# Attention followed by a Silu layer pair: a new order of loads, shifts and exponentials for the first batch

## The chip, the cores and the metric

The kernel runs on one core of a Trainium2 chip. The metric is the device time of one execution in microseconds; it was 334.84 (median of three runs, 333.54 to 335.08) before the change. A core has TensorE (PE, matrix products; its weight loads are shown as PEld), VectorE (DVE), ScalarE (ACT), GpSimd (POOL) and SyncE (SP). Transfers between memory and the core's SBUF run on 16 DMA engines; POOL and SP issue them here.

## The reference

Eight batches of eight heads, 576 positions, 64 features a head. Heads 0 to 3 see the 32 positions up to their own ("plain"), heads 4 to 7 every fourth position of the last 128 ("dilated"). The output of the attention, all heads of a position side by side (512 wide), goes through a layer of 2048 with h * sigmoid(h), and back to 512.

```python
scores = scale * np.matmul(q, k.transpose(0, 1, 3, 2))
mask_plain = (rel >= 0) & (rel < window)                       # window = 32
mask_dil = (rel >= 0) & (rel < window * dilation) & (rel % dilation == 0)   # dilation = 4
scores = np.where(masks[None, :, :, :], scores, -1000000000.0)
scores = scores - np.max(scores, axis=-1, keepdims=True)
attn = np.exp(scores)
attn = attn / (np.sum(attn, axis=-1, keepdims=True) + 1e-09)
x = np.matmul(attn, v)            # then (batch, position, head * feature)
h = x @ w_in
g = h * (1.0 / (1.0 + np.exp(-h)))
out = (g @ w_out).astype(np.float32)
```

## The kernel before

All products are in 16 bits with 32-bit sums. For each batch the kernel does attention in two kinds, z = 0 (plain heads) and z = 1 (dilated heads, as four classes of positions). Queries come in blocks of 32, each against a stretch of 64 keys. The steps of one kind are functions: `transpose` or `transpose0` (q and k turned by PE, copied out of PSUM by `copy`), `scores` or `scores0` (products, then on DVE the mask and the negated row maximum), `shift` (DVE adds the maximum, so that one exponential does for all blocks), `exps` (ACT: one exponential if `shift` was called, otherwise one for each of 8 to 12 blocks, each with a read of its row sum), `normal` (DVE: row sums if shifted, reciprocal, product), `turn` and `turned` (PE turns the weights, a copy brings them back), `values` or `values0` (products with v), `finish` or `finish0` (copies into xT). Then come layer 1 (`layer1`, `layer1_part`: products with w_in, Silu on ACT into gT) and layer 2 (`layer2_first`, `layer2`: products with w_out, a DVE copy, a store by SP).

Batch 0 is special. It runs in two parts of positions: part 0 is positions 0 to 255, part 1 the rest. `load_qk0`, `transpose0`, `scores0`, `values0`, `finish0` and `layer1_part` take the part. Its first half is written out by hand at the end of the kernel. The second half is placed by `plan_of(0)` between the pieces of layer 1: `at(s, fn, ...)` puts a call at step s, and `plan(s)` calls what stands there. Layer 1 of part 0 has steps -16 to -1 (a pair of f tiles each two steps), part 1 has 0 to 15, layer 2 has 16 to 31; the calls for batch 1 stand there too. In this way the program order of each engine is fixed. An engine takes its instructions in this order, and one that waits holds back those behind it.

The values are held in `vw`, one tile for each of two batches. Its rows 64 to 127 (KB to P) hold v as loaded, with 36 column blocks for the plain heads (h * 9 + m) and 16 for each of three dilated groups. Rows 32 to 63 and 0 to 31 hold the same shifted by 32 and 64 rows. `shift_v` makes them, in the parts `FIRST` (column blocks m 0 to 3 of the plain heads, first dilated group: what part 0 needs), `REST`, or `ALL`. For batch 0 the kernel before does this with seven DMAs on SP.

All loads of q, k, v, w_in and w_out are issued by POOL, since they change the type from 32 to 16 bits. Their order is: `load_qk0(0)`, the identity and band masks (POOL's own work), `load_qk0(1)`, v of batch 0, first dilated group and plain heads (L123, L136), w_in chunk 0 (L173), v's second and short groups (L123, L131), w_in chunks 1, 2, 3, the eight transfers of `load_qk(1)` (L102), `clear_v(1)` (memsets, L187 to L190), w_out chunks 0 and 1 (L179), `load_v(1)`, w_out chunks 2 and 3, and `load_qk(2)` (L102).

PSUM is held as two tiles `big` of two banks (fillers, batch 0's scores, h, o) and four tiles `ps` of one. `keep_busy` (L795) runs products of the identity with itself, whose results nobody reads: 96 of 32 columns at the start, 12 and 6 of 128 columns before and after the first values. `layer2_first` (L632 on) holds four output tiles t as halves of two `big` tiles, `o2[t // 2][:, t % 2]`, goes through four rounds c of four f tiles each, and stores t in the last round with `store` (L650).

Of the kernel before, what the change touches and what calls it, by code (L numbers as in the profile page):

```python
# [27 lines left out]
def kernel(  # L28
# [112 lines left out]
    def shift_v(b, queue, parts):  # L141

        vw = vws[b % 2]
        f = vw[:, 0:NP].rearrange("p (h m) d -> p h m d", h=HH)
        for m0, m1, n in parts:
            queue.dma_start(
                out=vw[W:KB, NP + n.start * ND : NP + n.stop * ND],
                in_=vw[KB : KB + W, NP + n.start * ND : NP + n.stop * ND],
            )
            if n.stop == 2:  # L150
                queue.dma_start(
                    out=vw[0:W, NP + ND : NP + 2 * ND], in_=vw[KB + W : P, NP : NP + ND]
                )
            queue.dma_start(out=f[W:KB, :, m0:m1], in_=f[KB : KB + W, :, m0:m1])
            l0 = max(m0, 1)
            queue.dma_start(out=f[0:W, :, l0:m1], in_=f[KB + W : P, :, l0 - 1 : m1 - 1])

    FIRST, REST, ALL = (0, 4, slice(0, 1)), (4, NM, slice(1, 2)), (0, NM, slice(0, 2))

# [9 lines left out]
    qk0 = {}  # L169
    FC = DFF // 4  # L170

    def load_w_in(c):
        nc.gpsimd.dma_start(  # L173
            out=w_in16[:, :, c * FC : (c + 1) * FC],
            in_=moe_w_in[:, c * FC : (c + 1) * FC].rearrange("(c p) f -> p c f", p=P),
        )

    def load_w_out(c):
# [88 lines left out]
    def to_classes(a, which, i, t0, t, copy):  # L267

        e, n = t.shape[1], t.shape[3]
        dst, i0 = ((a["qC"], 0), (a["kC"], W))[which]  # L270
        i0 += t0 // DIL
        copy(
            dst[:, 2 * i : 2 * i + 2, :, i0 : i0 + n * e].rearrange("d h r (p e) -> d (h r) p e", e=e),
            t.rearrange("d e m p -> d m p e"),
        )

    def transpose0(part, hp, which, copy):

# [4 lines left out]
        if hp >= HP // 2:  # L283
            t = t.rearrange("d (e m) p -> d e m p", m=4)
            for h in (0, 1):
                for u in range(0, UR, 2):
                    nc.tensor.transpose(
                        t[:, u // DIL, 2 * h + u % DIL // 2, :],
                        src[0:n, 2 * hp + h, u : u + 2, :].rearrange("p u d -> p (u d)"),
                        ident[0:n, 0:n],  # L290
                    )
            return to_classes(a, which, hp - HP // 2, t0, t, copy)
        for u in range(UR):
            for hi in (0, 1):
                nc.tensor.transpose(  # L295
                    t[hi * D : hi * D + D, u, :], src[0:n, 2 * hp + hi, u, :], ident[0:n, 0:n]
                )
        o = (a["qT"][:, hp], a["kT"][:, hp, W:])[which][:, t0 : t0 + n * UR]
        copy(o.rearrange("d (p u) -> d p u", u=UR), t.rearrange("d u p -> d p u"))

    def score(b, hp, hi, j, dst):

# [285 lines left out]
    def finish(b, z, copy=nc.vector.tensor_copy):  # L588
        a = att(b)
        run = QB * (DIL if z else 1)  # L590
        for e in (0, 1):
            copy(  # L592
                a["xT"][:, 2 * z : 2 * z + 2, 0:NS].rearrange("d n (m e c) -> d n m e c", e=2, c=run)[:, :, :, e, :],
                a["x", z][e].rearrange("d n (m c) -> d n m c", c=run),
            )
        for e in (0, 1):
            last_finish(b, z, e, copy)


    def layer1(b, f):  # L600
# [32 lines left out]
    def layer2_first(plan):  # L633

        o2 = [big.tile([P, 2, DM], F32, tag="big", name=f"o_0_{i}") for i in (0, 1)]
        for c in range(4):
            for t in range(4):
                plan(NFF + 4 * c + t)
                o = o2[t // 2][:, t % 2]
                for f in range(4 * c, 4 * c + 4):  # L640
                    nc.tensor.matmul(  # L641
                        o, gT[:, f, t * P : (t + 1) * P], w_out16[:, f, :],
                        start=(f == 0), stop=(f == NFF - 1),
                    )
                if c == 3:
                    store(o, t * P, f"ob_0_{t}")
# [37 lines left out]
        for which in (1, 0):  # L684
            at(step, transpose, b, z, which, both)

    def later(at, b, z, steps):

        for hi in (0, 1):
            at(steps[hi], normal, b, z, hi)  # L690
        for fn in (turn, turned):
            for hi in (0, 1):
                at(steps[2], fn, b, z, hi)
        at(steps[3], values, b, z)
        at(steps[3], finish, b, z)

    def plan_of(b):
        ev = {}
# [8 lines left out]
        if b == 0:  # L707
# [21 lines left out]
            at(14, shift_v, 1, nc.sync, (ALL,))  # L729
            at(15, load_qk, 3)  # L730
            at(15, load_v, 2)
            at(15, shift_v, 2, nc.gpsimd, (ALL,))
            all_exps(1, 1)
            for hi in (0, 1):
                at(17, exps, 1, 0, hi)
            later(at, 1, 1, (18, 20, 24, 26))
            later(at, 1, 0, (22, 25, 28, 30))
        elif b == 1:
            at(16, load_v, 3)
            at(16, shift_v, 3, nc.gpsimd, (ALL,))  # L740
            transposes(at, 2, 0, 4)
            transposes(at, 2, 1, 10)
            transposes(at, 3, 0, 15)
# [10 lines left out]
        else:  # L754
            if b + 2 < B:
                at(16, load_v, b + 2)
                at(16, shift_v, b + 2, nc.gpsimd, (ALL,))
            if b + 1 < B:
                if b == 2:
                    for n in (0, 1):  # L760
# [24 lines left out]

    def transposes0(part, z, copies):
        for which in (1, 0):
            for i in (0, 1):
                transpose0(part, 2 * z + i, which, copies[which])

    def keep_busy(n, c=P):

        busy = big.tile([P, 2, 512], F32, tag="big", name=f"busy_{c}")
# [36 lines left out]
    keep_busy(6)  # L830
    load_qk(2)

    for b in range(B):
# [47 lines left out]
```

## Time and profile before

The execution that was profiled has a span of 331.3 us from the first to the last instruction; the runs' times, which hold what lies around the span as well, have a median of 334.84. The page gives no other time for the profiled execution. The granted clock of TensorE is 1.000 over the span.

| engine | busy us | share of the span | instructions |
|---|---|---|---|
| PE | 313.2 | 95% | 5346 |
| PE weight loads | 206.7 | 62% | 5346 |
| DVE | 180.5 | 54% | 377 |
| ACT | 214.9 | 65% | 714 |
| POOL | 86.0 | 26% | 144 |

The chain of work that ended last is 88% PE, 4% each DVE and ACT, 2% each "issue" (time in which the engine waited for nothing that the profile shows) and DMA. In order of time, the beginning of the kernel is:

| us | what |
|---|---|
| 1.32, 2.02 | POOL issues the loads of k and q of part 0 |
| 3.25 to 5.9 | PE runs 96 fillers |
| 5.93, 7.09 | PE turns k and q of the dilated heads, as each lands |
| 7.94 | first scores |
| 13.30 | PE turns part 1 of the dilated heads |
| 22.85 to 25.87 | first values, with a gap of 1.76 |
| 26.48 | layer 1 begins |
| 31.49 | values of part 1, dilated heads (step -8) |
| 48.02 | layer 2 begins |
| 69.71 | layer 1 of batch 1 begins |

Times are read from the order of instructions on each engine. A line of such a view has the start, the duration of the whole group, the engine, the line of the code, the operation, the tiles written and read, the shape and how many there are; the brackets give the idle time before it and what released it.

### The profile page before, as it was taken

The numbers are of one execution on the slowest core, as the hardware profiler recorded it, in microseconds if no ns is written. First come the engines' busy times: TensorE is split into PE (matmuls) and PEld (weight loads), VectorE is DVE, ScalarE is ACT, GpSimd is POOL, SyncE is SP. The second block draws the span as 40 slices with busy tenths as digits, with TensorE's granted clock in tenths as the row PEclk, the third lists the DMA queues.
The fourth block names the chain that finished last, engine by engine and source line by source line (L and its number), as shares of the span: only waits on it lengthen the run. The fifth ranks groups of instructions, "written<-read, shape, count | busy, mean of one in ns | idle before, by whom it ended". The sixth has DMA issues, their size and how long they took to land.

```text
span 331.3 us, 12192 instructions
## 1 busy us (share of the span) xinstructions
PE 313.2 (95%) x5346; PEld 206.7 (62%) x5346; DVE 180.5 (54%) x377; ACT 214.9 (65%) x714; POOL 86.0 (26%) x144
## 2 busy tenths in 40 slices
PE   5579998989999999999999999999999999999995
PEld 4458764457745677467845677467745676468644
DVE  5687378746678744774557444774557442530011
ACT  2566669136699957995699357995699357826300
POOL 8445745645400560047004520051000000000000
PEclk9999999999999999999999999999999999999999
DMA  6999999999911984188504980184001100110021
GB/s 90 181 215 194 145 204 219 170 221 121 158 38 65 138 132 81 66 103 160 88 34 98 175 140 2 65 105 102 4 34 65 65 2 3 63 65 2 0 96 63
DMA packets 45141, 32.90 MB, mean 99 GB/s; under 512 B 21824, under 2 KB 39744, under 8 KB 45088
## 3 DMA queue, kind: packets, MB, share of 16 engines
q0 software_dynamic: 38752, 21.74, 47.8%
q1 hardware_dynamic: 6336, 10.39, 8.8%
q8 instruction: 41, 0.67, 0.8%
q14 instruction: 12, 0.10, 0.1%
HBM read 37.75 MB, written 9.44 MB: 142 GB/s over the span
## 4 chain that ended last, share of the span: by engine, by line
PE 88%; DVE 4%; ACT 4%; issue 2%; DMA 2%; POOL 0%; POOLq 0%
PE h L605 34%; PE o L665 31%; PE h L624 5%; PE t L259 3%; ACT pe L458 3%; PE pt L483 3%; PE x L516 2%; PE o L641 2%; PE s L317 2%; DMA n<-in_q_dram 2%; PE s L305 1%; PE t L295 1%; DVE pn L474 1%; PE busy L795 1%; PE xs L579 1%
## 5 line engine op out<-in xcount | busy, mean ns | idle before, releaser
L613 ACT ACTIVATE gT<-h 128x576 f16<-128x576 f32 x112 | 72.8, 650 | 73.0 <-PE h L605 72.3
L665 PE MATMUL o<-w_out,gT 128*128 128x512 f16 (+1 forms) x528 | 115.8, 373 | 0.5 <-DVE ob_last L674 0.5
L605 PE MATMUL h<-xT,w_in 128*128 128x288 f16 x896 | 115.4, 286 | 0.0
L605 PEld LDWEIGHTS <-w_in 128*128 128x128 f16 x896 | 85.7, 98 | 22.9
L458 ACT ACTIVATE pe<-ms,nm 128x64 f32<-128x64 f32 x262 | 87.0, 334 | 0.6 <-DVE nm L430 0.5
L665 PEld LDWEIGHTS <-gT 128*128 128x128 f16 x528 | 50.1, 98 | 53.6 <-issue 0.7
L650 DVE COPY ob<-o 128x512 f32<-128x512 f32 x35 | 24.1, 689 | 53.2 <-PE o L665 50.7
L458 ACT ACTIVATION_READ_ACCUMULATOR pe<-ms,nm 128x1 f32 x262 | 49.1, 187 | 0.0
L414 DVE SCALAR_TENSOR_TENSOR ms<-s,mask 128x512 f32<-128x512 f32 x28 | 19.2, 687 | 37.4 <-PE ss L305 19.3
L123 POOL DMA_DIRECT2D vw<-in_v_dram x16 | 10.0, 632 | 86.7 <-PE x L516 86.4
L474 DVE TENSOR_TENSOR pn<-pe,r 128x640 f16<-128x640 f32 (+2 forms) x32 | 25.3, 792 | 1.1
L592 DVE CAST xT<-x 128x512 f16<-128x512 f32 x28 | 18.0, 686 | 11.2 <-PE xs L579 11.2
L430 DVE TENSOR_REDUCE nm<-ms 128x10 f32<-128x640 f32 (+1 forms) x28 | 22.0, 787 | 1.0
L102 POOL DMA_DIRECT2D n<-in_q_dram x28 | 16.4, 601 | 13.4 <-DMA w_in<-in_moe_w_in_dram 4.9
L102 POOL DMA_DIRECT2D n<-in_k_dram x28 | 16.5, 602 | 8.6 <-DMA w_in<-in_moe_w_in_dram 2.8
L491 DVE COPY ptT<-pt 128x640 f16<-128x640 f16 (+2 forms) x30 | 13.1, 473 | 9.8 <-PE pt L483 9.7
L624 PE MATMUL h<-xT,w_in 128*128 128x256 f16 (+1 forms) x128 | 18.3, 298 | 0.0
L641 PE MATMUL o<-w_out,gT 128*128 128x512 f16 x64 | 15.1, 379 | 2.0 <-DVE ob L650 2.0
L631 ACT ACTIVATE gT<-h 128x512 f16<-128x512 f32 (+1 forms) x16 | 10.4, 650 | 8.1 <-PE h L624 7.9
L624 PEld LDWEIGHTS <-w_in 128*128 128x128 f16 x128 | 12.3, 102 | 3.7 <-issue 0.2
L483 PE MATMUL pt<-ident,pn 128*128 128x128 f16 x152 | 12.2, 224 | 1.1 <-DVE pn L474 1.1
L259 PEld LDWEIGHTS <-n 64*64 64x64 f16 (+1 forms) x840 | 10.0, 101 | 4.5 <-issue 3.9
(85 smaller groups left out, 267.9 us busy)
## 6 DMA issues: line engine op xcount, KB each, us to landing
out_dram<-ob SPq DMA_DIRECT2D x35, 256.0 KB, 2.0
n<-in_k_dram POOLq DMA_DIRECT2D x28, 144.0 KB, 5.6
n<-in_q_dram POOLq DMA_DIRECT2D x28, 144.0 KB, 5.9
vw<-in_v_dram POOLq DMA_DIRECT2D x8, 288.0 KB, 6.0
vw<-in_v_dram POOLq DMA_DIRECT2D x16, 128.0 KB, 4.4
w_in<-in_moe_w_in_dram POOLq DMA_DIRECT2D x4, 512.0 KB, 12.1
w_out<-in_moe_w_out_dram POOLq DMA_DIRECT2D x4, 512.0 KB, 9.9
vw<-vw POOLq DMA_DIRECT2D x12, 128.0 KB, 3.1
```

Source lines behind the costliest of these rows:

```text
L102: nc.gpsimd.dma_start(out=qk[b, z, which][i * HF : i * HF + UPS[z]].rearrange("p h u d -> p h (u d)"), in_=src[b, h : h + 2].rearrange("h ...
L259: nc.tensor.transpose(dst, w, ident[r, r])
L430: nc.vector.tensor_reduce(out=nm[:, 0:w], in_=ms[:, 0:w], axis=AX.X, op=ALU.max, negate=True)
L458: nc.scalar.activation(pe[:, t, :], ms[:, t, :], AF.Exp, bias=nm[:, t : t + 1], accum_out=l[:, t : t + 1],)
L474: nc.vector.tensor_tensor(pn[:, 0:w], a["pe", z, hi][:, 0:w], r[:, 0:w, None].broadcast_to([P, w, KB]), ALU.mult)
L483: nc.tensor.transpose(t[:, i, :], a["pn", z, hi][:, 2 * i : 2 * i + 2].rearrange("p t c -> p (t c)"), ident)
L605: nc.tensor.matmul(h[:, half, 0:HS], w_in16[:, c, f * P : f * P + P], xT[:, c, half * HS : half * HS + HS], start=(c == 0), stop=(c == MC ...
L613: nc.scalar.activation(gT[:, f, s0 : s0 + S].rearrange("p (a c) -> p a c", a=2), h[:, :, 0:HS], AF.Silu)
L624: nc.tensor.matmul(h[:, i, 0 : c1 - c0], w_in16[:, c, (f + i) * P : (f + i + 1) * P], xT[:, c, c0:c1], start=(c == 0), stop=(c == MC - 1),)
L641: nc.tensor.matmul(o, gT[:, f, t * P : (t + 1) * P], w_out16[:, f, :], start=(f == 0), stop=(f == NFF - 1),)
L650: nc.vector.tensor_copy(ob, o)
L665: nc.tensor.matmul(o[:, part, 0:m] if last else o[:, 0], gT[:, f, t * P : (t + 1) * P], w_out16[:, f, part * m : (part + 1) * m] if last e ...
```

## The change

It moves and alters the steps of the beginning, and a few of those in the steps of batch 0 and 1:

- v of batch 0, plain heads: one transfer for each head, in two pieces, "plain first" (column blocks 0 to 3) and "plain rest". w_in comes in three transfers, chunks 0, 1, and 2 with 3.
- `shift_v` takes the copy to use. For batch 0 this is `nc.gpsimd.tensor_copy`: `FIRST` (three copies) stands on POOL behind w_in's first two transfers, `REST` (four copies) behind `load_qk(1)` and `clear_v(1)`.
- `transpose0` turns a whole kind into one PSUM tile, with one copy.
- The fillers are 7 products of 512 columns at the start, and none after.
- Part 0's dilated heads are shifted before their exponential too (`shift(0, 1, 0)`), all of batch 0's exponentials come before the first Silu, with `exps(0, 0, 1)` ahead of the last `finish0`, and more copies are on ACT.
- `layer2_first` takes its tiles in the order 0, 2, 1, 3.
- For batch 1, the dilated heads' transposes stand at step 6 (2 before), their scores and shifts at step 10 (8 before), and the plain heads' `turned` and `finish` copies go half to ACT.

```diff
+        for name, m0, m1 in (("plain first", 0, 4), ("plain rest", 4, NM)):
+            for h in range(HH) if name in pieces else ():
+                nc.gpsimd.dma_start(
+                    out=vw[KB:P, h * NM + m0 : h * NM + m1],
+                    in_=v[b, h, m0 * KB : m1 * KB].rearrange("(m r) d -> r m d", r=KB),
+                )
...
-    load_v(0, ("first", "plain"))
-    load_w_in(0)
-    load_v(0, ("second", "short"))
-    shift_v(0, nc.sync, (FIRST, REST))
-    for c in range(1, 4):
-        load_w_in(c)
+    load_v(0, ("first", "plain first"))
+    load_w_in(0, 1)
+    load_w_in(1, 2)
+    shift_v(0, nc.gpsimd.tensor_copy, (FIRST,))
+    load_v(0, ("second", "plain rest", "short"))
+    load_w_in(2, 4)
...
-    def transpose0(part, hp, which, copy):
+    def transpose0(part, z, which, copy):
...
-        t = ps.tile([P, UR, n], F16, tag="ps", name=f"t{which}_0{part}_{hp}")
+        t = ps.tile([P, 2 * UR, n], F16, tag="ps", name=f"t{which}_0{part}_{z}")
...
-            for t in range(4):
-                plan(NFF + 4 * c + t)
+            for x, t in enumerate((0, 2, 1, 3)):
+                plan(NFF + 4 * c + x)
...
-            transposes(at, 1, 1, 2)
-            at(8, scores, 1, 1)
+            transposes(at, 1, 1, 6)
+            at(10, scores, 1, 1)
             for hi in (0, 1):
-                at(8, shift, 1, 1, hi)
+                at(10, shift, 1, 1, hi)
...
-            later(at, 1, 0, (22, 25, 28, 30))
+            later(at, 1, 0, (22, 25, 28, 30), both)
...
+    def keep_busy(n):
+
+        busy = big.tile([P, 2, 512], F32, tag="big", name="busy")
         for _ in range(n):
-            nc.tensor.matmul(busy[:, 0, 0:c], ident, ident[:, 0:c], start=True, stop=True)
+            nc.tensor.matmul(
+                busy[:, 0].rearrange("p (a c) -> p a c", c=P), ident,
+                ident[:, None, :].broadcast_to([P, 4, P]), start=True, stop=True,
+            )
 
     load_qk(1)
     clear_v(1, nc.gpsimd)
+    shift_v(0, nc.gpsimd.tensor_copy, (REST,))
     load_w_out(0)
     load_w_out(1)
     load_v(1)
     load_w_out(2)
     load_w_out(3)
-    keep_busy(96, W)
+    keep_busy(7)
     transposes0(0, 1, (act, dve))
     scores0(1, 0)
-    transposes0(0, 0, (act, dve))
+    shift(0, 1, 0)
+    transposes0(0, 0, (act, act))
     exps(0, 1, 0)
     scores0(0, 0)
-    transposes0(1, 1, (act, dve))
+    transposes0(1, 1, (act, act))
     exps(0, 0, 0)
     normal(0, 1, 0)
     scores0(1, 1)
     turn(0, 1, 0)
     turned(0, 1, 0, act)
+    shift(0, 1, 1)
     transposes0(1, 0, (act, act))
     normal(0, 0, 0)
+    exps(0, 1, 1)
+    values0(1, 0)
+    scores0(0, 1)
     turn(0, 0, 0)
     turned(0, 0, 0, act)
-    shift(0, 1, 1)
-    exps(0, 1, 1)
-    scores0(0, 1)
+    finish0(1, 0, (act, act))
     shift(0, 0, 1)
-    keep_busy(12)
-    values0(1, 0)
-    finish0(1, 0, (dve, act))
     values0(0, 0)
+    exps(0, 0, 1)
     finish0(0, 0, (dve, act))
-    exps(0, 0, 1)
-    keep_busy(6)
     load_qk(2)
```

More of the change, by code (lines that the diff above doesn't have):

```diff
@@ L139, in load_v, with shift_v @@
             )
-    def shift_v(b, queue, parts):
+        for name, m0, m1 in (("plain first", 0, 4), ("plain rest", 4, NM)):
[4 more added lines that the diff above has]
+                )
+    def shift_v(b, copy, parts):
         vw = vws[b % 2]
@@ L145, in shift_v @@
         for m0, m1, n in parts:
-            queue.dma_start(
+            copy(
                 out=vw[W:KB, NP + n.start * ND : NP + n.stop * ND],
@@ L150, in shift_v @@
             if n.stop == 2:
-                queue.dma_start(
+                copy(
                     out=vw[0:W, NP + ND : NP + 2 * ND], in_=vw[KB + W : P, NP : NP + ND]
                 )
-            queue.dma_start(out=f[W:KB, :, m0:m1], in_=f[KB : KB + W, :, m0:m1])
+            copy(out=f[W:KB, :, m0:m1], in_=f[KB : KB + W, :, m0:m1])
             l0 = max(m0, 1)
-            queue.dma_start(out=f[0:W, :, l0:m1], in_=f[KB + W : P, :, l0 - 1 : m1 - 1])
+            copy(out=f[0:W, :, l0:m1], in_=f[KB + W : P, :, l0 - 1 : m1 - 1])
     FIRST, REST, ALL = (0, 4, slice(0, 1)), (4, NM, slice(1, 2)), (0, NM, slice(0, 2))
@@ L170, with load_w_in @@
     FC = DFF // 4
-    def load_w_in(c):
+    def load_w_in(c0, c1):
         nc.gpsimd.dma_start(
-            out=w_in16[:, :, c * FC : (c + 1) * FC],
-            in_=moe_w_in[:, c * FC : (c + 1) * FC].rearrange("(c p) f -> p c f", p=P),
+            out=w_in16[:, :, c0 * FC : c1 * FC],
+            in_=moe_w_in[:, c0 * FC : c1 * FC].rearrange("(c p) f -> p c f", p=P),
         )
@@ L281, in transpose0 @@
         t0, n = ((0, PA), (SA, PB))[part]
-        t = ps.tile([P, UR, n], F16, tag="ps", name=f"t{which}_0{part}_{hp}")
-        if hp >= HP // 2:
-            t = t.rearrange("d (e m) p -> d e m p", m=4)
-            for h in (0, 1):
+        t = ps.tile([P, 2 * UR, n], F16, tag="ps", name=f"t{which}_0{part}_{z}")
+        if z:
+            t = t.rearrange("d (e m) p -> d e m p", m=8)
+            for h in range(HH):
                 for u in range(0, UR, 2):
@@ L288, in transpose0 @@
                         t[:, u // DIL, 2 * h + u % DIL // 2, :],
-                        src[0:n, 2 * hp + h, u : u + 2, :].rearrange("p u d -> p (u d)"),
+                        src[0:n, HP + h, u : u + 2, :].rearrange("p u d -> p (u d)"),
                         ident[0:n, 0:n],
                     )
[L292 to L299, printed above, removed]
+            dst, i0 = ((a["qC"], 0), (a["kC"], W))[which]
+            i0 += t0 // DIL
+            e = UR // DIL
+            copy(
+                dst[:, :, :, i0 : i0 + n * e].rearrange("d h r (p e) -> d (h r) p e", e=e),
+                t.rearrange("d e m p -> d m p e"),
+            )
+            return
+        t = t.rearrange("d (i u) p -> d i u p", i=2)
+        for i in (0, 1):
+            for u in range(UR):
+                for hi in (0, 1):
+                    nc.tensor.transpose(
+                        t[hi * D : hi * D + D, i, u, :], src[0:n, 2 * i + hi, u, :], ident[0:n, 0:n]
+                    )
+        o = (a["qT"], a["kT"][:, :, W:])[which][:, :, t0 : t0 + n * UR]
+        copy(o.rearrange("d i (p u) -> d i p u", u=UR), t.rearrange("d i u p -> d i p u"))
     def score(b, hp, hi, j, dst):
@@ L586, in last_finish, with finish @@
             copy(xT[:, 2 + e, NS:S], xs.rearrange("d a c -> d (a c)"))
-    def finish(b, z, copy=nc.vector.tensor_copy):
+    def finish(b, z, copies=(nc.vector.tensor_copy, nc.vector.tensor_copy)):
         a = att(b)
@@ L591, in finish @@
         for e in (0, 1):
-            copy(
+            copies[e](
                 a["xT"][:, 2 * z : 2 * z + 2, 0:NS].rearrange("d n (m e c) -> d n m e c", e=2, c=run)[:, :, :, e, :],
@@ L596, in finish @@
         for e in (0, 1):
-            last_finish(b, z, e, copy)
+            last_finish(b, z, e, copies[e])
     def layer1(b, f):
@@ L685, in transposes, with later @@
             at(step, transpose, b, z, which, both)
-    def later(at, b, z, steps):
+    def later(at, b, z, steps, copies=(nc.vector.tensor_copy, nc.vector.tensor_copy)):
         for hi in (0, 1):
             at(steps[hi], normal, b, z, hi)
-        for fn in (turn, turned):
-            for hi in (0, 1):
-                at(steps[2], fn, b, z, hi)
+        for hi in (0, 1):
+            at(steps[2], turn, b, z, hi)
+        for hi in (0, 1):
+            at(steps[2], turned, b, z, hi, copies[hi])
         at(steps[3], values, b, z)
-        at(steps[3], finish, b, z)
+        at(steps[3], finish, b, z, copies)
     def plan_of(b):
@@ L722, in plan_of @@
             at(-2, last_finish, 0, 0, 1)
[L723 to L724 removed]
+            transposes(at, 1, 1, 6)
+            at(10, scores, 1, 1)
             for hi in (0, 1):
[L726 removed]
+                at(10, shift, 1, 1, hi)
             transposes(at, 1, 0, 13)
             at(17, scores, 1, 0)
[L729 removed]
+            at(14, shift_v, 1, nc.sync.dma_start, (ALL,))
             at(15, load_qk, 3)
             at(15, load_v, 2)
[L732 removed]
+            at(15, shift_v, 2, nc.gpsimd.dma_start, (ALL,))
             all_exps(1, 1)
@@ L736, in plan_of @@
             later(at, 1, 1, (18, 20, 24, 26))
-            later(at, 1, 0, (22, 25, 28, 30))
+            later(at, 1, 0, (22, 25, 28, 30), both)
         elif b == 1:
             at(16, load_v, 3)
-            at(16, shift_v, 3, nc.gpsimd, (ALL,))
+            at(16, shift_v, 3, nc.gpsimd.dma_start, (ALL,))
             transposes(at, 2, 0, 4)
@@ L756, in plan_of @@
                 at(16, load_v, b + 2)
-                at(16, shift_v, b + 2, nc.gpsimd, (ALL,))
+                at(16, shift_v, b + 2, nc.gpsimd.dma_start, (ALL,))
             if b + 1 < B:
@@ L787, in transposes0 @@
         for which in (1, 0):
[L788 to L793, printed above, removed]
+            transpose0(part, z, which, copies[which])
+    def keep_busy(n):
+        busy = big.tile([P, 2, 512], F32, tag="big", name="busy")
         for _ in range(n):
-            nc.tensor.matmul(busy[:, 0, 0:c], ident, ident[:, 0:c], start=True, stop=True)
+            nc.tensor.matmul(
+                busy[:, 0].rearrange("p (a c) -> p a c", c=P), ident,
+                ident[:, None, :].broadcast_to([P, 4, P]), start=True, stop=True,
+            )
     load_qk(1)
     clear_v(1, nc.gpsimd)
+    shift_v(0, nc.gpsimd.tensor_copy, (REST,))
     load_w_out(0)
```

## The prediction

> **What bounds the kernel now.** I read the busy time by stages first, then the waits, then the order of time on GpSimd (POOL) and TensorE (PE). The windows view, columns PE, weight loads, DVE, ACT, POOL (busy us, instructions), clock, DMA share, GB/s:
>
> ```profile
> 0.00:26.50 26.50, 16.04 (x531) 13.82 (x532) 17.03 (x46) 12.86 (x49) 14.09 (x28) 1.00 1.15 166
> 26.50:48.10 21.60, 21.60 (x430) 16.39 (x429) 14.10 (x30) 13.58 (x21) 14.06 (x21) 1.00 1.22 172
> 48.10:66.50 18.40, 16.01 (x300) 8.28 (x298) 14.00 (x31) 10.70 (x41) 9.26 (x15) 1.00 1.14 197
> 107.00:331.30 224.30, 220.31 (x3385) 143.05 (x3382) 109.60 (x223) 147.79 (x492) 36.30 (x60) 1.00 0.38 72
> ```
>
> From 26.5 us on PE has work nearly without a gap, so whatever stops PE later than that goes straight to the end. Before 26.5 PE is idle for 10 us. The change touches only the first 70 us; what follows is the same code, and I count it at nothing. Who stops PE is in the waits of PE (us in total, times, longest):
>
> ```profile
> PE t L295 <- issue: 2.9, 2, 2.0
> PE o L641 <- DVE ob L650: 2.0, 2, 1.2
> PE x L542 <- issue: 1.8, 1, 1.8
> PE s L305 <- issue: 0.8, 1, 0.8
> ```
>
> The waits for "issue" come at 10.44, 17.94, 23.33 and 49.27. Between the first three PE runs 128 matmuls each, that is 256 instructions with the weight loads, and each stall ends about 6.3 us after the one before (12.43, 18.89, 25.09). I read them as code blocks of 256 instructions, fetched through busy DMA engines: the packets of the queue "instruction" fall in 9-10, 16-17 and 22-23 us. That POOL's transfers hold one another shows in its timeline:
>
> ```profile
> 11.73 0.76 POOL L173 DMA_DIRECT2D w_in<-in_moe_w_in_dram  x1 [2.29 <-DMA n<-in_k_dram]
> 13.13 0.74 POOL L173 DMA_DIRECT2D w_in<-in_moe_w_in_dram  x1 [0.64 <-DMA n<-in_q_dram]
> ...
> 29.06 0.59 POOL L102 DMA_DIRECT2D n<-in_q_dram  x1 [2.20 <-DMA w_in<-in_moe_w_in_dram]
> 29.64 0.33 POOL L187 MEMSET vw<- 32x256 f16 x1
> 29.89 0.97 POOL L188 MEMSET vw<- 32x1024 f16 x1
> 30.91 1.94 POOL L190 MEMSET vw<- 32x1024 f16 x2
> 32.80 1.50 POOL L179 DMA_DIRECT2D w_out<-in_moe_w_out_dram  x2
> ```
>
> Count POOL's transfers: the 11th (w_in chunk 1) waits for the 3rd (k, part 1), the 12th for the 4th, the 21st (last of load_qk(1)) for the 13th (w_in chunk 3). Each waits for the one eight before it. That is the rule that matters here.
>
> **The change, part by part.** *Order of the stores (L636).* In the last round of layer2_first, t=1 waits for the copy of t=0 out of the same tile, t=3 for that of t=2:
>
> ```profile
> 64.20 0.69 DVE L650 COPY ob<-o 128x512 f32<-128x512 f32 x1 [0.32 <-PE o L641]
> 64.94 1.02 PE L641 MATMUL o<-w_out,gT 128*128 128x512 f16 x4 [0.78 <-DVE ob L650]
> ...
> 68.85 1.02 PE L641 MATMUL o<-w_out,gT 128*128 128x512 f16 x4 [1.23 <-DVE ob L650]
> ```
>
> With 0,2,1,3 the other tile's 4 matmuls (0.88 us) stand between, longer than a copy (0.69). ACT now takes half of the turned and finish copies of this stage, so DVE has room; ACT is idle there (11.38 us before its Silu at 70.89). Gain 0.78 + 1.23 = 2.0 us. If DVE were late after all, up to 1.2 of it would stay.
>
> *Scores of batch 1 at step 10, not 8; transposes at 6, not 2.* One f pair later is 1.14 us (16 matmuls in 2.28). DVE's chain of masks, maxima and shifts ran 42.65 to 47.51, then its kT and qT copies ended at 48.84, and PE's scores at L305 began at 48.98. Moved by 1.14, the copies end at 50.0, where the 0.83 of "issue" stood until 50.11. The scores (0.7) then end near 50.8, against 50.64: the stage loses 0.2 if the fetch moves off (the chain of DVE to the turn at 57.84 moves with the scores); the ends are -0.8, DVE catching up, and +1.1, the fetch falling behind it. I take +0.2.
>
> *The beginning on PE.* 114 filler matmuls become 7 of 512 columns: at the spacing of 0.213 us for 256 columns seen at 27 us, 7 x 0.43 = 3.0, so 3.25 to 6.25, behind which k (5.9) has just landed. One shift (0.69 on DVE) and one row sum (0.69) replace eight exponentials with their reads: 12.91 to 15.57 on ACT becomes about 0.63. Copies of 512 elements replace pairs of 256 (0.6 for 0.74 on ACT), but wait for all transposes. Part 1's loads still land at 11.7 and 13.1, so its 32 transposes end near 13.6. 214 fewer instructions put the first block's end in the scores (1,1) and the second in the scores (0,1). With 6.4 us a block, counted from where the block before is entered (9.5), they are let go near 15.9 and 22.3. Then scores (0,1) end at 22.95, DVE follows with 0.69 + 0.28 + 0.82 + 0.82, ACT with the exponential (0.75) and, since that now stands ahead of it, the last xT copy (0.37): layer 1 starts at 26.7, against 26.5 before. With no stall of the fetch it is 24.0. So this part is worth -2.5 to +0.2 at the start of layer 1. It is worth nothing if something holds PE behind it, and something does.
>
> *POOL.* SP's seven shift transfers go (their 5.6 to 6.7 us to landing were hidden), and seven copies enter POOL's own row. Its transfers are now: 1-4 q and k; 5 first; 6-9 plain first; 10, 11 w_in chunks 0, 1; three copies; 12 second; 13, 14 short; 15-18 plain rest; 19 w_in chunks 2 and 3 in one; 20-27 load_qk(1); then the memsets and the other four copies; then w_out. The 11th still waits for k to 11.73. The copies wait for v first (SP went on at 13.86) and plain first (all 288 KB had landed at 16.23, so 128 KB by 14.9). No POOL copy is in the trace. Nearest rows: POOL's memset of 32x1024, 0.97; its affine_select, 0.287 for 128 and 0.229 for 64 elements, which at that slope makes 1.1 for 1024. Low end 0.55 (DVE sets the same bytes in 0.485), high end 1.94 (twice the memset, for reading and writing); I take 1.1, on the two POOL rows. First three copies: 13.9 to 16.95 (2816 elements). Then 0.64 + 2 x 0.6 + 4 x 0.65 = 4.4 of issuing, so the 19th goes out at 21.4. Its 1 MB lands as two chunks did: 2.2 each (16.2 to 18.4) to 3.0 each (23.0 to 29.0), and 1.3 for the start (the first load's packets move a good us after issue): 27.1 to 28.7, say 28.2. The 27th waits for it: 28.4 to 29.0. Memsets 3.2 (29.64 to 32.80): 32.2. Two class copies: 34.4.
>
> Values (1,1) at step -8 need these two, and PE, which takes its work in order, stands there with layer 1 behind it. Before, PE began this work at 31.56. PE would reach it 5.1 us after layer 1's start, at 29.1 to 31.8, so it waits, and loses 34.4 - 31.56 = 2.85. The two plain copies (1.4 each) end at 37.2, just as PE comes to values (0,1), 2.7 us on. w_out goes out 4.4 later (37.2 for 32.8): the last chunk landed before 53.9, is needed at 63.3, so that slack of 9 us hides it; batch 1's v (landed 44, needed 60) likewise.
>
> **Sum**: +2.85 - 2.0 + 0.2 = +1.05 on a span of 331.3, so 332.35. The median of the runs, 334.84, lies 3.54 above the span; the page gives no other time of the profiled execution. 335.9.
>
> **Rivals.** *Slow copies* (slower): from 1.3 us per 1024 elements both pairs of copies hold PE. At 1.5, the first three end 1.1 later, the class pair takes 0.8 more, the plain pair 3.75 against 2.7 of PE's work, so 1.05 more, and PE, stopped twice, pays its slow restart: +3.75, 339.6. At 1.94 it is 343. For it: two accesses a value; against it: the affine_select reads and writes too. The Trainium skill, "GPSIMD Engine Reference", section "Performance versus the Vector engine", gives 1.8 cycles at 1.2 GHz as the best of an unrolled loop; by that, an estimate of 1.54 us a copy, this rival would hold. No POOL copy before the change can test it.
>
> *Slow restart of PE alone.* At 26.4 to 27.6 six matmuls of layer 1 start, then 8, then 13; later 12 in the same 1.2 us, while the granted clock stays 1.00 in the row. The first 24 took 3.73 us; at 8 in 0.98 they take 2.94. So a fresh start costs 0.8 here, with 18 fillers just before it. Paid again after the wait: 336.7. Against: PE stands still 2.6 to 5 us, and stalls of 0.8 at 49.27 left no such mark. The Trainium skill, "TensorE: Matmul & The Clock Gate", section "HAM oscillation — how this bites in real kernels", asks for no idle gap over about 3.4 us, else half rate for as long; it speaks against taking fillers away, and by it the estimate is 1.7 instead of 0.8, 337.6. The trace has the halved spacing, but not in the clock column.
>
> *The gate is open* (faster): copies at 0.55 and w_in landing in 4.4. Then the 19th goes at 19.9, lands at 25.6, the class copies end near 30.7, and the beginning decides: PE reaches step -8 at 30.7 to 31.8. -0.5 - 2.0 + 0.2 = -2.3, 332.5. For it: SP's traffic, 0.46 MB (seven transfers of 48 to 80 KB), is gone from the DMA engines.
>
> **How the numbers follow.** Forecast 0.42 (its own range 334.5 to 337.3, from w_in's landing and the DVE stage), slow copies 0.23, slow restart 0.12, open gate 0.23. The range 332.4 to 340.4 takes the open gate, and slow copies up to 1.55. About 0.5% (1.7 us) is what a measurement can tell from no change, so 333.2 to 336.5 is the same: half of the forecast's cases and some of the restart's and the open gate's, 0.36. Faster 0.20 (open gate). Slower 0.44: slow copies, most of the restart, the forecast's upper part.
>
> **What would show it.** PE's first values L542 of the second pair wait for POOL's copies (not for "issue") and start near 34.4; POOL's last load of batch 1 waits for w_in; the row of a POOL copy of 32x1024 near 1.1; no PE wait on ob L650; layer 1 starting between 24 and 27. I am wrong if the REST copies are done by 31, if the transfers do not hold one another by eights, or if layer 1 starts after 29.

## The result, and the profile after

The changed kernel takes 343.68 us (median of 4 runs, 342.53 to 345.16), the kernel before 334.21 in the same session: a ratio of 1.0278, with a 95% interval from 1.0245 to 1.0311. The span of the profiled execution is 342.8, for 331.3 before. By the medians the change costs 9.5 us; the two profiled executions lie 11.5 apart, so some 2 us of what the profiles show below belong to these two executions alone. The forecast was 335.9.

The windows view of the same stretches of time as before, which now hold other parts of the work (columns PE, weight loads, DVE, ACT, POOL, granted clock, DMA share, GB/s), and PE's waits:

```profile
0.00:26.50 26.50, 16.24 (x434) 11.83 (x435) 20.47 (x46) 14.02 (x34) 20.86 (x37) 1.00 0.98 130
26.50:48.10 21.60, 14.61 (x212) 11.00 (x212) 4.75 (x14) 6.23 (x11) 14.82 (x19) 0.84 0.83 134
48.10:66.50 18.40, 16.78 (x337) 10.11 (x330) 15.32 (x28) 14.75 (x49) 9.20 (x16) 1.00 1.35 211
```

```profile
PE x L557 <- POOL vw L157: 7.0, 1, 7.0
PE pt L498 <- DVE pn L489: 3.0, 4, 1.5
PE h L620 <- DVE ob L665: 2.7, 1, 2.7
PE h L639 <- ACT xT L570: 1.6, 1, 1.6
...
PE h L620 <- issue: 0.6, 1, 0.6
```

In the stretch in which PE had no gap before, it is now busy for 14.61 of 21.60 us, and the mean clock is 0.84. Of the waits on a code block ("issue") one of 0.6 us is left, at 99.8 us, and no wait of o for ob; in their place stand 7.0 us for a POOL copy, and 2.7 for an output buffer. POOL's order of time shows the first:

```profile
21.69 0.84 POOL L179 DMA_DIRECT2D w_in<-in_moe_w_in_dram  x1
...
31.05 0.59 POOL L102 DMA_DIRECT2D n<-in_q_dram  x1 [4.49 <-DMA w_in<-in_moe_w_in_dram]
...
34.89 1.03 POOL L152 COPY vw<-vw 32x1024 f16<-32x1024 f16 x1
35.96 1.03 POOL L157 COPY vw<-vw 32x1024 f16<-32x1024 f16 x1
```

The last load of batch 1 waits for w_in's chunks 2 and 3, the memsets stand behind it, and the REST copies behind these. PE and its clock at this place (timeline, then windows):

```profile
24.32 4.53 PE L639 MATMUL h<-xT,w_in 128*128 128x256 f16 x24 [1.64 <-ACT xT L570]
29.02 1.04 PE L639 MATMUL h<-xT,w_in 128*128 128x256 f16 x8
37.05 0.64 PE L557 MATMUL x<-ptT,vw 64*64 64x32 f16 x32 [6.99 <-POOL vw L157]
37.80 1.89 PE L639 MATMUL h<-xT,w_in 128*128 128x256 f16 x8
```

```profile
30.00:31.00 1.00, 0.06 (x1) 0.00 (x0) 0.00 (x0) 0.60 (x1) 0.00 (x0) 1.00 1.14 203
36.00:37.00 1.00, 0.00 (x0) 0.00 (x0) 0.00 (x0) 0.00 (x0) 0.99 (x1) 0.50 0.00 0
39.00:40.00 1.00, 1.00 (x9) 0.82 (x7) 0.00 (x0) 0.28 (x1) 1.00 (x2) 0.50 0.00 0
```

Layer 1 starts 2.2 us sooner than before (24.32 for 26.48), then PE stands still, the clock goes to 0.50 after some 4.7 us of it (at 34.8 us; it is back at 1.00 at 41.6), and the eight products that took 1.04 us take 1.89. The second new wait is at the end of layer 2's first tiles:

```profile
71.90 0.69 DVE L665 COPY ob<-o 128x512 f32<-128x512 f32 x1 [0.72 <-PE o L656]
72.62 6.67 SPq L666 DMA_DIRECT2D out_dram<-ob  x4
...
78.24 0.69 DVE L665 COPY ob<-o 128x512 f32<-128x512 f32 x1 [3.14 <-DMA out_dram<-ob]
78.99 4.77 PE L620 MATMUL h<-xT,w_in 128*128 128x288 f16 x24 [2.67 <-DVE ob L665]
```

The four copies now come closer together. There are three output buffers (tile pool o32), so the fourth copy waits until the first store has landed, 5.5 us after its issue, and the second f tile of batch 1 waits for the PSUM tile that this copy empties. The 24 products after it take 4.77 us, at half clock for part of it (the clock is at 0.50 from 79.1 to 82.6 us). In the kernel before, the same store was issued at 64.9 and landed 3.75 us later, at 68.7, and the fourth copy came after that:

```profile
64.92 6.04 SPq L651 DMA_DIRECT2D out_dram<-ob  x4
...
69.91 0.69 DVE L650 COPY ob<-o 128x512 f32<-128x512 f32 x1 [1.11 <-PE o L641]
```

Where the 11.5 us of span went:

| stretch | before | after | difference |
|---|---|---|---|
| to the values of step -8 | 31.49 | 37.05 | +5.6 |
| from there to the start of layer 2 | 16.53 | 19.60 | +3.1 |
| to the start of batch 1's layer 1 | 21.69 | 18.51 | -3.2 |
| to its first transposes | 4.01 | 8.53 | +4.5 |
| to the end | 257.6 | 259.1 | +1.5 |

### The profile page after: what moved, and what is told of

Same layout as the page of the kernel before. It is cut to its first block, busy times and chain, and to the rows that moved or that the text cites. A ratio compares the mean times of both kernels' runs of the same rounds, so it can differ in the third digit from the quotient of the medians.

```text
span 342.8 us, 11953 instructions
## 1 busy us (share of the span) xinstructions
PE 315.9 (92%) x5239; PEld 205.5 (60%) x5239; DVE 180.3 (53%) x370; ACT 215.5 (63%) x700; POOL 97.0 (28%) x157
## 4 chain that ended last, share of the span: by engine, by line
PE 76%; DMA 9%; POOL 7%; DVE 3%; ACT 2%; issue 1%; POOLq 0%; DVEq 0%
PE h L620 33%; PE o L680 30%; PE t L265 3%; DMA w_out<-in_moe_w_out_dram 3%; DMA w_in<-in_moe_w_in_dram 3%; PE x L531 2%; DMA vw<-in_v_dram 2%; PE pt L498 2%; ACT pe L473 2%; DMA out_dram<-ob 2%; PE o L656 2%; PE s L320 1%; POOL vw L142 1%; PE s L332 1%; POOL n L114 1%
## 5 line engine op out<-in xcount | busy, mean ns | idle before, releaser
L620 PE MATMUL h<-xT,w_in 128*128 128x288 f16 x896 | 117.4, 289 | 3.3 <-DVE ob L665 2.7
L620 PEld LDWEIGHTS <-w_in 128*128 128x128 f16 x896 | 86.3, 99 | 27.8 <-issue 3.8
L473 ACT ACTIVATE pe<-ms,nm 128x64 f32<-128x64 f32 x254 | 84.3, 334 | 0.1
L473 ACT ACTIVATION_READ_ACCUMULATOR pe<-ms,nm 128x1 f32 x254 | 47.6, 188 | 0.0
L489 DVE TENSOR_TENSOR pn<-pe,r 128x640 f16<-128x640 f32 (+2 forms) x32 | 26.0, 812 | 1.1
L646 ACT ACTIVATE gT<-h 128x512 f16<-128x512 f32 (+1 forms) x16 | 10.4, 651 | 18.7 <-PE h L639 18.6
L639 PE MATMUL h<-xT,w_in 128*128 128x256 f16 (+1 forms) x128 | 20.6, 323 | 1.6 <-ACT xT L570 1.6
L506 DVE COPY ptT<-pt 128x640 f16<-128x640 f16 (+2 forms) x29 | 12.7, 472 | 12.0 <-PE pt L498 11.9
L639 PEld LDWEIGHTS <-w_in 128*128 128x128 f16 x128 | 13.5, 110 | 6.1 <-DMA vw<-in_v_dram 1.1
L498 PEld LDWEIGHTS <-pn 128*128 128x128 f16 x152 | 10.3, 101 | 6.1 <-DVE pn L489 3.6
```

Source lines behind the costliest of these rows:

```text
L473: nc.scalar.activation(pe[:, t, :], ms[:, t, :], AF.Exp, bias=nm[:, t : t + 1], accum_out=l[:, t : t + 1],)
L489: nc.vector.tensor_tensor(pn[:, 0:w], a["pe", z, hi][:, 0:w], r[:, 0:w, None].broadcast_to([P, w, KB]), ALU.mult)
L498: nc.tensor.transpose(t[:, i, :], a["pn", z, hi][:, 2 * i : 2 * i + 2].rearrange("p t c -> p (t c)"), ident)
L620: nc.tensor.matmul(h[:, half, 0:HS], w_in16[:, c, f * P : f * P + P], xT[:, c, half * HS : half * HS + HS], start=(c == 0), stop=(c == MC ...
L639: nc.tensor.matmul(h[:, i, 0 : c1 - c0], w_in16[:, c, (f + i) * P : (f + i + 1) * P], xT[:, c, c0:c1], start=(c == 0), stop=(c == MC - 1),)
```

## The experiments

Theory A: the place of the REST copies in POOL's row holds PE, with a slow restart behind it, and the new order of the tiles trades one wait for another. All ratios are to the kernel before, run on the same chip in the same session, with 95% intervals.

| kernel | ratio | interval |
|---|---|---|
| the changed kernel | 1.0278 | 1.0245 to 1.0311 |
| REST copies ahead of load_qk(1) | 1.0029 | 0.9983 to 1.0076 |
| shifts as SP's DMAs | 0.9950 | 0.9914 to 0.9986 |
| four output buffers | 1.0179 | 1.0113 to 1.0244 |
| fillers inside the wait | 1.0347 | 1.0277 to 1.0416 |
| w_in ahead of v's small pieces | 1.0295 | 1.0239 to 1.0351 |
| old order of tiles | 1.0254 | 1.0217 to 1.0290 |
| REST early, fillers | 1.0047 | 1.0020 to 1.0074 |
| REST early, four buffers | 0.9923 | 0.9886 to 0.9961 |
| REST early, fillers, four buffers | 0.9913 | 0.9880 to 0.9946 |
| SP's DMAs, fillers, four buffers | 0.9919 | 0.9897 to 0.9942 |
| before, new order of tiles | 0.9972 | 0.9950 to 0.9993 |
| before, new order, four buffers | 0.9946 | 0.9926 to 0.9965 |

**The copies' place.** One line moved:

```diff
+    shift_v(0, nc.gpsimd.tensor_copy, (REST,))
     load_qk(1)
     clear_v(1, nc.gpsimd)
-    shift_v(0, nc.gpsimd.tensor_copy, (REST,))
```

> The changed kernel with one move: the four REST copies on GpSimd stand ahead of load_qk(1) and clear_v(1), not behind them. Theory A (the place of these copies in GpSimd's row holds PE): v's rest has landed by about 24, the copies end near 28.6, PE reaches step -8 near 30 and does not wait; the 7.0 us wait and the 2.2 us of half clock behind it go, so 334.5 us, 9 less than the changed kernel. Rival B (the copies as such are too slow or slow DVE, wherever they stand): PE still waits 2 us or more at step -8, 340 or above. Rival C (the missing fillers cost the clock): the half clock at the start of layer 1 stays and the time falls by less than 7.

335.56 us, a ratio lower by 0.025, or 8.3 us. From its timeline:

```profile
23.11 1.54 POOL L157 COPY vw<-vw 32x1024 f16<-32x1024 f16 x1
...
26.00 1.25 POOL L162 COPY vw<-vw 32x1280 f16<-32x1280 f16 x1
```

```profile
24.83 5.28 PE L639 MATMUL h<-xT,w_in 128*128 128x256 f16 x24 [2.48 <-ACT xT L570]
...
31.41 0.45 PE L557 MATMUL x<-ptT,vw 64*64 64x32 f16 x32
```

The copies are done at 27.25, PE does not wait at step -8, and batch 1's loads, now behind them, come early enough. So A holds and B falls. But layer 1, though it starts 1.7 us sooner than before the change, comes to step -8 at the same time (31.41 for 31.49): its first 24 products take 5.28 us, for 3.88 before. That part of C is right; its other part, a fall of less than 7 us, is not.

**The shifts by SP.**

```diff
-    shift_v(0, nc.gpsimd.tensor_copy, (FIRST,))
+    shift_v(0, nc.sync.dma_start, (FIRST,))
...
-    shift_v(0, nc.gpsimd.tensor_copy, (REST,))
+    shift_v(0, nc.sync.dma_start, (REST,))
```

> The changed kernel with batch 0's shifts, FIRST and REST, as DMAs on SyncE again, issued in the same places of the text. Theory A: GpSimd no longer stops for copies, w_in's last chunks go out near 16 and land near 26, REST lands before PE needs it; layer 1 starts near 26 since FIRST lands 5 to 6 us after its issue; 335 us. Rival B (the copies as such): the same time, so this run alone does not tell A from B, but with the early copies it does: by A both are within 1.5 us of each other, by B this one is 5 us or more ahead. Rival C (fillers): 340 or more here too.

332.97 us, a ratio lower by 0.008 (2.6 us) than with early copies: between the 1.5 us of A and the 5 us of B, with intervals that just touch. C falls. With fillers and four buffers in both (below), copies on POOL and transfers by SP give the same time, so the copies as such are not shown to cost anything; what made the 2.6 us here is open. A's times for w_in were wrong: with SP's shifts, fillers and four buffers the last chunks went out at 20.4, not near 16, since that transfer waited for w_in chunk 1, eight before it, and they landed at 30.5. PE still did not wait at step -8.

**Four output buffers.**

```diff
-    o32 = ctx.enter_context(tc.tile_pool(name="o32", bufs=3))
+    o32 = ctx.enter_context(tc.tile_pool(name="o32", bufs=4))
```

> The changed kernel with four output buffers instead of three. In its profile the fourth store of layer2_first waits 3.1 us for the DMA that empties the first one's buffer, and PE behind it 2.7 us, then runs 24 products at half clock (4.77 for 2.94 us). Theory A (the new order of the tiles trades the wait on the PSUM tile for a wait on the output buffer): 4.5 us less than the changed kernel, 339.2. Rival D (DVE or the DMA queue is late anyway and PE stops there for another reason): within 1 us of the changed kernel.

340.15 us, a ratio lower by 0.0099, or 3.3 us, of 4.5 expected. The wait of h for ob is gone, and 32 products at the start of batch 1 run through in 4.09 us. D falls.

**Fillers inside the wait.**

```diff
+            at(-8, keep_busy, 30)
             at(-8, values0, 1, 1)
```

> The changed kernel with 30 fillers of 512 columns (6.5 us at full clock) in front of the values of step -8, where PE stands still for 7.0 us. Theory A (the wait is GpSimd's, and the half clock from 34.9 to 41.3 is the price of standing still): the values still start near 37.05, but the clock stays at 1.00 and the stretch behind is 2.2 us shorter: 341.5. Rival E (half clock comes from something else, such as the power state): no gain, or a loss if the fillers overrun: 343.7 or more.

346.06 us: slower, not faster. The near part went as A said. The values start at 36.91, the clock stays at 1.00, the next eight products take 1.05 us, and the last stretch of part 0 starts at 41.21, for 43.43. The wait of h for ob is gone too, since the first store landed in 2.9 us, for 5.5. But the 2.2 us and more are lost again in the transposes for batch 1, and layer 2 begins at 59.56, for 56.65:

```profile
51.65 0.64 PE L265 MATMUL t<-ident,n 64*64 64x64 f16 x33 [0.80 <-DMA vw<-in_v_dram]
55.12 0.27 PE L265 MATMUL t<-ident,n 64*64 64x64 f16 x3 [2.83 <-issue]
55.32 4.45 PE L639 MATMUL h<-xT,w_in 128*128 128x320 f16 x16
```

Sixty instructions more (30 products and their weight loads) put the end of a code block into a dense run of small products; PE waits 2.83 us for the next block, and the clock, at 0.50 again, makes the 16 products after it take 4.45 us for 2.35. So at step -8 the half clock is the price of standing still, and the part of E that put it down to something else falls; the time of the whole kernel did not show the gain, since the edit moved another stall.

**w_in ahead of the small pieces.** The 1 MB transfer took 9.1 us from issue to landing, where the prediction had 6.8.

```diff
+    load_w_in(2, 4)
     load_v(0, ("second", "plain rest", "short"))
-    load_w_in(2, 4)
```

> The changed kernel with w_in chunks 2 and 3 issued ahead of v's second, short and plain-rest pieces, not behind them. In the changed kernel the 1 MB took 9.1 us from issue to landing, and the core's DMA moved only 70 GB/s at 21 to 23 us, while the small pieces went, and 205 from 25 on. Theory A (small runs ahead of w_in delay it, and each transfer of GpSimd waits for the one eight before): w_in is the 12th now, goes out at 17.3 and lands near 24.5; the 20th, the first load of batch 1, waits for it; load_qk(1) ends near 29.5 and not 31.6, the class copies near 34.9 and not 37.0; 2 us less than the changed kernel, 1.021 of before. Rival I (w_in's transfer needs 9 us wherever it stands): it lands at 26.4, the class copies end at 36.8, and nothing is gained, 1.027. Rival K (no rule of eights: only the last load waits for w_in): the first load of batch 1 goes out without a wait near 22.

```profile
17.40 0.75 POOL L179 DMA_DIRECT2D w_in<-in_moe_w_in_dram  x1
...
26.73 1.21 POOL L102 DMA_DIRECT2D n<-in_k_dram  x2 [4.12 <-DMA w_in<-in_moe_w_in_dram]
...
34.66 1.03 POOL L152 COPY vw<-vw 32x1024 f16<-32x1024 f16 x1
```

343.51 us: nothing gained. The rule of eights is shown: w_in is the 12th now, and the 20th transfer, batch 1's first, waits for it. But w_in needed 8.8 us here too, as rival I said. In both kernels the core's DMA moved little in the first four microseconds after the issue (143, 87, 83 and 160 GB/s from 17 to 21 us here), and some 200 then; why is open. In the changed kernel the two transfers of 0.5 MB took about as long (8.8 and 9.0 us) as the one of 1 MB. My reason, the small runs ahead of it, is not enough.

**The order of the tiles.** First undone in the changed kernel:

```diff
-            for x, t in enumerate((0, 2, 1, 3)):
-                plan(NFF + 4 * c + x)
+            for t in range(4):
+                plan(NFF + 4 * c + t)
```

> The changed kernel with the old order of output tiles (0, 1, 2, 3) and three buffers. Theory A (in the changed kernel the order takes away 2.0 us of waiting on PSUM tiles and brings 2.7 us of waiting on a buffer and 1.8 us of half clock): 2.5 us less than the changed kernel, 1.020 of before. Rival (the wait for the buffer comes from the crowded DMA queue and stays with either order): 1.028 or more.

343.21 us. The ratio lies between the two, and its interval overlaps the changed kernel's: undecided by time. In the profile PE waits 2 x 0.78 us for ob again, no wait on a buffer is left, and the waits on code blocks come to 3.0 us, for 0.6; 1.3 of them stand at the products of batch 1. Then the order alone, in the kernel before, and with four buffers:

> The kernel before with the new order of output tiles (0, 2, 1, 3) alone, and three output buffers. Theory A (the wait on the PSUM tile goes, and a wait on an output buffer comes): PE no longer waits 2.0 us for the copies; the fourth copy, due near 68, waits for the first store to land, 4.3 to 5.5 us after 65, so PE waits about 1 to 1.5 us at the second f tile of batch 1: 0.5 us gained, 0.998 of before. Rival G (the order is a clean gain of 2.0, and the wait of the changed kernel comes from its other lateness): 0.994. Rival H (the order itself loses): 1.005 or more.

> The kernel before with the new order of output tiles and four output buffers. Theory A: no wait on a PSUM tile, none on an output buffer, 2.0 us gained: 0.994 of before. Rival G: the same as the run with three buffers. Rival H: no gain.

0.9972 and 0.9946, both as A said. The two intervals overlap; what tells the runs apart is the profile. Three buffers, then four:

```profile
70.92 0.69 DVE L650 COPY ob<-o 128x512 f32<-128x512 f32 x1 [1.52 <-DMA out_dram<-ob]
71.67 3.10 PE L605 MATMUL h<-xT,w_in 128*128 128x288 f16 x24 [1.07 <-DVE ob L650]
```

```profile
67.89 1.28 DVE L650 COPY ob<-o 128x512 f32<-128x512 f32 x2
68.63 4.08 PE L605 MATMUL h<-xT,w_in 128*128 128x288 f16 x32 [0.34 <-DVE ob L650]
```

The gain was there: 1.8 us by the ratio with four buffers. With three, 0.9 of it is left here. In the changed kernel four buffers gave 3.3 us, more than the order gains, and there PE also restarts at half clock.

**Fillers again, and the best together.**

```diff
     scores0(0, 1)
+    keep_busy(2)
     turn(0, 0, 0)
...
     values0(0, 0)
+    keep_busy(5)
     exps(0, 0, 1)
```

> The kernel with the REST copies early, and fillers again: 2 products of 512 columns behind the scores (0,1) and 5 behind the values (0,0), 2.6 us at the start where PE stands still for 2.5 us anyway; the output buffers stay three. In the run without them the first 24 products of layer 1 took 5.28 us, before the change 3.88, at full clock 2.94. Theory F (the fillers taken away cost clock at the start of layer 1): the 24 take 4 us or less, step -8 comes 1.2 us sooner, 334.3 us or 0.999 of before. Rival (the phase of the clock's window decides, not the fillers): still near 5.3, and no gain.

335.39 us, no gain. The first 24 products took 4.40 us, between F's 4 and the rival's 5.3, and step -8 came 0.3 us sooner (31.10 for 31.41), not 1.2. Layer 2 began at 48.62, for 49.75 without the fillers, most of it because a wait of 1.07 us on a code block did not come here. The next place took it back:

```profile
71.83 3.10 PE L620 MATMUL h<-xT,w_in 128*128 128x288 f16 x24 [3.51 <-DVE ob L665]
```

PE came sooner, and the first store took longer to land: 6.3 us, for 3.1 in the profiled execution without the fillers, in which PE did not wait for a buffer at all. What the longer executions of that kernel waited for (they go up to 339.49, the profiled one took 333.92) is not shown. So four buffers with this, without the fillers, and with SP's shifts:

> The kernel with the REST copies early on GpSimd and the fillers (2 and 5 of 512 columns), now with four output buffers. With three, PE waited 3.5 us at 68.3 for a buffer, longer than in any other run, since it came there sooner. Theory A: this wait goes and 3.5 us with it, 331.9 us, 0.993 of before, level with SyncE's shifts (0.992). Rival (the gain is given back at a later place once more): 0.998 or above.

> The kernel with the REST copies early and four output buffers, but without the fillers before layer 1. Theory F (fillers save clock at the start of layer 1): 0.7 to 1.2 us slower than the same kernel with fillers, 0.996 of before. Rival (the phase of the clock's window, which differs from run to run, decides): the two are within 0.5 us, with intervals that overlap.

> The kernel with batch 0's shifts as DMAs on SyncE, with the fillers (2 and 5 of 512 columns) and four output buffers: what the runs so far say should be best. Without fillers and with three buffers it was 0.995 of before. By theories A and F it gains 1.2 us of clock at the start of layer 1 and the 1.2 us that PE waited for an output buffer: 0.988 of before, 330.6 us. If the blocks of code now end at a worse place, a stall of 1 to 2.8 us comes in their stead: 0.992 to 0.996.

331.41, 332.13 and 331.51 us. All three beat both kernels; the last fell short of its 0.988. REST early and four buffers together lower the changed kernel's ratio by 0.0355, or 11.9 us, alone by 8.3 and 3.3: two costs that add up. From the profiles with and without fillers:

```profile
25.30 3.82 PE L639 MATMUL h<-xT,w_in 128*128 128x256 f16 x24
```

```profile
23.93 5.28 PE L639 MATMUL h<-xT,w_in 128*128 128x256 f16 x24 [1.80 <-ACT xT L570]
```

The fillers delay layer 1 by 1.4 and shorten its first 24 products by 1.5; the medians differ by 0.7 us, the ratios by 0.001 (0.3 us), with intervals that overlap. The clock records in the traces lean to the rival: the clock rises at 27.4 to 28.9 us in the three kernels with these fillers and at 27.5 to 30.9 in the changed kernel and those made from it without them. In the two kernels before with the new order, whose code is the same up to there, it rises at 31.1 and 28.2, and the 24 products took 5.14 and 3.61 us. So the moment differs from one execution to the next by more than the fillers could be seen to move it. Whether they gain is not settled.

## Why the prediction was wrong

- **The rule of eights, and the class copies holding PE at step -8: right.** The last load waits for w_in, and PE waits for L157. A POOL copy of 32x1024 took 1.03 us, for 1.1 taken from the memset and the affine_select. So the time near "slow copies" (343) came about without slow copies. Copies of 32x768 and 32x1280 took 0.82 and 1.25 us when nothing held them, so an element more costs 0.84 ns. The 1.8 cycles an element of the Trainium skill, "GPSIMD Engine Reference", section "Performance versus the Vector engine", from which the prediction estimated 1.54 us, are not what this copy needs.
- **w_in's landing: mis-sized.** Taken as 28.2 from the spacing at which chunks had landed, it was 30.8; with it, step -8 came at 37.05, for 34.4. The transfer went out at 21.7, nearly as forecast (21.4), but took 9.1 us and not 6.8. The spacing of transfers in a full queue is not the time of one transfer from its issue; the row for that (12.1 us to landing for a chunk) was on the page.
- **The slow restart: at nothing in the sum, a rival with 0.12, and it came.** Standing still was sized as 2.6 to 5 us and was 7.0. The clock was at 0.50 from 34.8 to 41.6, and with the 0.7 us in which transposes waited for DVE the stretch behind step -8 grew by 3.1 us; the sum had nothing there (its 0.2 stood in layer 2). The price of a restart, read as 0.8 where fillers stood ahead, was 2.1: the stretch from 37.05 to 43.43 took 6.4 us, with fillers inside the wait 4.3. The rule of the Trainium skill, "TensorE: Matmul & The Clock Gate", section "HAM oscillation — how this bites in real kernels" (no gap over some 3.4 us, else half rate), agrees with this gap: the column falls to 0.50 some 4.7 us into it and stays there 4.5 us after PE goes on. But the length alone does not decide here: just after the 2.67 us of waiting for the buffer the clock fell too, while after 3.51 us (REST early, fillers) it stayed at 1.00. In the traces, between its first and its last change, the clock keeps a value for 3.41 us or a multiple of it (3.41 and 6.83 at half clock here), so it seems to matter as well when a gap falls; that is a reading of the records, not an experiment.
- **"Gain 0.78 + 1.23 = 2.0 us": the step that failed.** It named the wait that goes and did not ask what the copies wait for next. With copies 0.9 to 1.7 us apart, the fourth needs the buffer of the first, whose store is issued at 72.6 and lands 5.5 us later. The line `bufs=3` was in the code, and the rows of the kernel before gave the size: its fourth copy, at 69.9, comes 2.0 us sooner without the two waits, near 67.9, and the first store landed at 68.7, an estimate of 0.8 us of waiting. In the changed kernel it cost 2.7 us of waiting and 1.8 of half clock: layer 2 and what follows it lost 1.3 us, where the sum had a gain of 1.8 (2.0 less 0.2). How long the wait is depends on the store, which took 2.9 to 6.3 us to land in the runs.
- **The beginning: the price was wrong, the statement held.** Layer 1 began at 24.3, not 26.7, since no code block stalled PE there; that it is worth nothing while something holds PE behind it was right.
- **Behind 70 us "counted at nothing"**: besides the buffer's wait and half clock, 1.5 us were lost there, 0.6 of it in a wait on a code block at 99.8; the rest was not traced.

Set against the table, the errors are 2.7 us of w_in, 3.1 of restart and transposes, 4.5 of buffer and half clock, less 1.4 by which layer 2 itself gained more than forecast (3.2 for 1.8; a wait of 0.8 us on a code block went as well), and 1.5 at the end: 10.4, which with the forecast 1.05 makes the 11.5. No one of them makes the difference alone. The wait for POOL's copies, the mechanism on which the forecast rested, was there and was larger than forecast.

## What to carry to other kernels

A copy put on an engine that also issues transfers waits for every transfer ahead of it, and each of these may wait for an older one; count the transfers before placing it. When a wait is removed, look at once for the next shared thing: buffers in a pool, their stores, the code blocks. Judge an edit at the front of a long in-order chain only together with the buffers behind it: the same order of tiles gained or lost by what stood next.

## What the runs showed of the hardware that was not expected

- A POOL copy and a DVE product hold each other up. DVE's product of 128x768, started 0.28 us into the POOL copy at 26.00 (early copies), took 1.77 us; with no copy running it took 0.96 (SP's shifts, fillers, four buffers). Where the product started just ahead of a copy (REST early, fillers, four buffers), it took 0.96, and the copy of 32x1280 took 2.06 for 1.25:

```profile
26.28 1.77 DVE L489 TENSOR_TENSOR pn<-pe,r 128x768 f16<-128x768 f32 x1
```

```profile
26.12 0.96 DVE L489 TENSOR_TENSOR pn<-pe,r 128x768 f16<-128x768 f32 x1
```

```profile
25.41 0.96 DVE L489 TENSOR_TENSOR pn<-pe,r 128x768 f16<-128x768 f32 x1
```

```profile
25.42 2.06 POOL L160 COPY vw<-vw 32x1280 f16<-32x1280 f16 x1 [0.34 <-issue]
```

  The Trainium skill, "GPSIMD Engine Reference", section "Specifications", names contention of the shared SBUF interface with DVE instructions that have two SBUF inputs; these rows agree.
- The granted clock reads 1.00 at the start of some profiles while the products run at half pace: 6 or 7 products of 256 columns a microsecond at 25 to 28 us in the changed kernel, 14 and 12 in the two after. In the run with early copies it reads 0.50 there. The changed kernel's trace has no clock record before 27.9 us, that of the kernel before none before 28.8: the 1.00 ahead of them is no reading of the clock. The spacing of the products is the safer sign.
- Code blocks of 256 instructions: PE stalled 0.2 to 2.8 us at their ends. In the first 105 us of all traces they come after 223 products, or after 128 or a multiple of it more (up to six fewer, since some records are missing), so an edit that only adds or removes instructions moves them to other work.
